# Softcap attention and two MLPs on one core: another order of the first matmuls' end products, differences of their outputs taken inside them, and another order of the first attention steps

## The chip, the cores and the metric

The kernel runs on one core of one Trainium2 chip. The time is the device time of one execution in microseconds (us); the median of three runs of the kernel before is 1092.13 us (1091.44 to 1093.55). The trace comes from one profiled execution that took 1090.3 us, of which the span of the recorded instructions is 1087.7 us.

In the profile PE is the matmul engine (PEld its weight loads), DVE the vector engine, ACT the scalar engine, POOL and SP the two engines that here mostly issue transfers (DMAs).

## The reference

```python
def _attn_ref(q, k, v, cap):                    # q, k, v: (4, 12, 448, 64)
    scores = (1.0 / np.sqrt(64)) * np.matmul(q, k.transpose(0, 1, 3, 2))
    scores = cap * np.tanh(scores / cap)
    scores = scores - np.max(scores, axis=-1, keepdims=True)
    attn = np.exp(scores)
    attn = attn / (np.sum(attn, axis=-1, keepdims=True) + 1e-09)
    return np.matmul(attn, v)

def _moe_ref(x, w_in, w_out):                   # (1792, 768) x (768, 2048) x (2048, 768)
    h = np.maximum(x @ w_in, 0.0)
    return h * h @ w_out

def _moe2_ref(x, w_in, w_out):
    h = x @ w_in
    return (h * (1.0 / (1.0 + np.exp(-1.702 * h)))) @ w_out
```

The attention's output, laid out as 4 x 448 tokens by 12 x 64 columns, goes through the first and then the second of these layers. All data are 32-bit floats.

## The kernel before, in words

Every matmul input is split into a high and a low part, and a product is the sum of three matmuls: high by high, high by low, low by high. The splits are made on the chip: ACT copies the high part (of a weight `wh`, L1120; of an activation `form`, L1152), and DVE subtracts it for the low part (`wl`, L1121; `form`, L1153).

**Attention** takes 12 quads (two pairs of heads each) in four steps each, 48 steps in all, written out by `attn_step(s)`: transposes of q and k (`qps`, `kps`), scores (`sps`, L834), tanh (`tanhs`, ACT L847), exponentials (`exps`, ACT L851), and the sums over v of quads before (`vxps`, `vyps`, L867). `attn_loads(s)` issues the loads on the SP queue by the table LOADS (L1532), where a larger first number is an earlier step. Loads take a rotating buffer, so a load is also held until its buffer's last reader is done. While attention runs, weights for the layers are unpacked from the inputs' own format and written to scratch in memory; POOL's queue loads them (`wraw`) and writes them (`wsa`, `wsb`), SP's queue later reads them back (`wf`).

**The layers.** For each layer l (0, 1) and each pair of batches c (0, 1) there is a first matmul "a" (768 to 2048) and a second "b" (2048 to 768). Each is done in a form of matrix multiplication with seven products where the direct one has eight; the seven products' inputs are sums and differences of blocks, called forms. So "a" is 56 products (s, o), with s the form (1 to 7) and o the column block (0 to 7), of nine matmuls each; "b" is 21 products of 24 matmuls. PE runs a(0,0), b(0,0), a(0,1), b(0,1), a(1,0), b(1,0), a(1,1), b(1,1), one after the other; the first matmuls stand at 234 to 338, 446 to 546, 653 to 756 and 868 to 971 us. The first two products of b are interleaved with the last two of a.

**Around a product.** For product u the program writes: what is in the list `later` (DVE work, flushed just ahead of the product), the nine or 24 matmuls, the split of the weights of four products further on (W_AHEAD), a step of making forms (`x_step` for the next or current "a", `b_step` for "b"), then `after(u)`, which takes the outputs from PSUM, adds them up and applies the layer's curve, and last a slot of the background unpacking (A_WORK, B_WORK, in chunks). `in_order` (L1391) keeps this written order on every engine, so an instruction that waits also holds everything written behind it on its engine. The seven forms rotate in seven buffers.

**Forms of "a".** `x_step(l, c, 0)` to `(l, c, 4)` run in the last products of the b before. Steps 5, 6 and 7 (forms 3, 2 and 4) follow products k = 0, 1 and 2 of the new "a", whose products begin (1,0), (5,0), (6,0), (2,0), (7,0), (1,1). Each form is 128x1344: an ACT copy and a DVE subtraction.

**Forms of "b".** The outputs of "a" are the blocks g11, g12, g21 and g22. `b_step` makes the forms of b from them in three chunks of columns (1344, 1344, 896 wide), with wide DVE subtractions (L1269). The first form of each chunk is written behind products (5,7), (6,7) and (2,7) of "a", after their `after`.

**The start.** Step 0 writes the scores of both pairs, then both tanhs, then transposes of the second quad's k and q, where the q's (`qps`) wait until the k's (`kps`) have been read out of their PSUM bank, and only then the scores of step 1. The scalar `capt` comes by a DMA of ACT's own queue, ahead of ACT's q loads.

Of the kernel before, what the change touches and what calls it, by code (L numbers as in the profile page):

```python
# [677 lines left out]
def bounded_cap(ctx, tc, q, k, v, cap, w1, w2, w3, w4, out, over):  # L678

    nc = tc.nc  # L680
# [212 lines left out]

    def start_pair(b, p):
        prep_q(b, p, transposed(raw[b, p, "q"], "qps", ps_m.tile([P, 512], F32, tag="m", name="qps")))
        prep_k(b, p)

    def attn_step(s):
# [7 lines left out]
        for i, x in enumerate(now):  # L906
            if s == 0 and i:
                start_pair(*x)
            scores(*x, c)
            if c == TAIL and ahead:  # L910

                t = raw[(*ahead[0][1], "q" if i else "k")]
                more.append(transposed(t, "qps" if i else "kps", sc[(*x, c)][:, 1]))
        for x in now:
            tanhs(*x, c)
        for f, ps in zip((prep_k, prep_q), more):
            f(*ahead[0][1], ps)
        if s == 0:
            prep_k(*ahead[0][0])
# [9 lines left out]
        if c == 0 and ahead:  # L929
            prep_q(*ahead[0][0])  # L930
# [142 lines left out]
    def a_products(l, c):  # L1073
        for o in range(NJ):
            yield (1, o)
            yield (5, o)
            if o:
                yield (4, o - 1)
            yield (6, o)
            if o:  # L1080
                yield (3, o - 1)
            yield (2, o)
            yield (7, o)
# [139 lines left out]
    def x_step(l, c, step):  # L1223
# [15 lines left out]
        if step == 0:  # L1239
            get("t", left, 0)  # L1240
            get("u", right, 0)
            get("w", right, NX)
        elif step == 1:
            form(1, "t")
            sub("t", "u", "t")
        elif step == 2:
            form(5, "t")
            sub("u", "w", "u")
        elif step == 3:
            form(7, "u")  # L1250
            later.append(lambda: get("u", left, NX))
            sub("t", "w", "t")
        elif step == 4:
            form(6, "t")
        elif step == 5:
            form(3, "w")
        elif step == 6:
            form(2, "u")
            sub("t", "u", "t")
        else:  # L1260
            form(4, "t")

    def b_step(l, c, s, ch):
# [4 lines left out]
        def sub(o, x, y):  # L1268
            later.append(lambda: v_.tensor_tensor(o, x, y, ALU.subtract))  # L1269

        def form(src):
            split_form((l, c, "b", s, ch), src, n)

        if s == 1:
            form(g11)
        elif s == 2:
            form(g21)
            sub(g11, g12, g11)
            t = gt["t", ch] = wide("tl")[:, :n]
            sub(t, g22, g11)  # L1280
        elif s == 6:
            form(gt["t", ch])
            sub(g12, g22, g12)
        elif s == 7:
            form(g12)
            sub(g21, g21, gt.pop(("t", ch)))
        elif s == 4:
            form(g21)
        elif s == 5:
            form(g11)  # L1290
        else:
            form(g22)
# [47 lines left out]

    def after(u):
# [19 lines left out]
        elif s == 7:  # L1361
            keep("u3", ps("b"))
            if kind == "a":
                g = gt["22"][:, i]
                plus("u3", ps("e"), g)
                curve(l, g)
# [4 lines left out]
        elif s == 3 and kind == "a":  # L1371
            g = gt["12"][:, i]
            plus("u2", ps("e"), g)
            curve(l, g)
# [27 lines left out]
    nc.vector.memset(kz[0][:, TAIL], 0.0)  # L1402
    for t in kz[1:]:
        nc.gpsimd.memset(t[:, TAIL], 0.0)
    nc.scalar.dma_start(out=capt, in_=cap.rearrange("(o n) -> o n", o=1).to_broadcast([P, 1]))
# [47 lines left out]
    for u, (l, c, kind, s, i) in enumerate(seq):  # L1453
# [4 lines left out]
        product(u)  # L1458
        if u == 0:
# [19 lines left out]
        if kind == "b" and n < 7:  # L1479
            b_step(l, c, order[n], i)  # L1480
        after(u)
        k = place[kind]
        place[kind] += 1
        if kind == "a":
            if i == NJ - 1 and s in (5, 6, 2):
                b_step(l, c, 1, (5, 6, 2).index(s))
# [4 lines left out]
            elif k < 3:  # L1491
                x_step(l, c, k + 5)
# [3 lines left out]
            if w0 <= k < 7 * NJ - 2:  # L1496
                weight_slots(k - w0, 7 * NJ - 2 - w0, m)
# [34 lines left out]
LOADS = ((8, "q", 0), (8, "k", 1), (7, "q", 1), (10, "k", 0), (1, "v", 0), (1, "v", 1))  # L1532
KB = 4
QB = 3
RAWQ = lambda nc: nc.gpsimd
W_AHEAD = 4
A_WORK = {(0, 0): 17 - ATT_CHUNKS, (0, 1): 6, (1, 0): 7}
# [46 lines left out]
```

## Time and profile before

| what | us |
|---|---|
| median of three runs | 1092.13 (1091.44 to 1093.55) |
| the profiled execution | 1090.3 |
| its span of recorded instructions | 1087.7 |
| PE busy | 1050.3 (97%) |
| DVE busy | 825.1 (76%) |
| ACT busy | 685.3 (63%) |
| POOL busy | 279.9 (26%) |

The difference of 2.6 us between the profiled execution and its span lies ahead of the first and behind the last recorded instruction. PE is busy for all but 37 us of the span; idle time is counted from the modelled end of the matmul before. Read the layers by stage: a stage lasts 85 to 120 us, and inside it PE waits only at a few places.

### The profile page before, as it was taken

How to read it: one execution, taken by the hardware profiler on the slowest of the kernel's cores; microseconds unless marked ns; L12 is line 12 of the kernel's file. 1: busy time of each engine (PE TensorE's matmuls, PEld its weight loads, DVE VectorE, ACT ScalarE, POOL GpSimd, SP SyncE). 2: the span in 40 equal slices, each digit the busy share in tenths (PEclk: the TensorE clock that was granted, in tenths of full speed). 3: DMA queues.
4: the chain of work that ended last, by engine and by line, in shares of the span. 5: the costliest groups of instructions: out<-in, count | busy, mean ns of one | idle time of the engine just before them, and what ended most of it. 6: DMA issues, size and time to landing. Idle time of an engine off the chain costs nothing.

```text
span 1087.7 us, 17044 instructions
## 1 busy us (share of the span) xinstructions
PE 1050.3 (97%) x5887; PEld 865.8 (80%) x5887; DVE 825.1 (76%) x1156; ACT 685.3 (63%) x1072; POOL 279.9 (26%) x422
## 2 busy tenths in 40 slices
PE   6999989999999999999999999999899999999997
PEld 4444534468999999899999998999899889998996
DVE  2686888876879976966798777878994975579854
ACT  5887869975767565566765646667555455564551
POOL 1223333322541022123202313442113400001033
PEclk9999999999999999999999999999999999999999
DMA  5798898956996487688846767997344543333443
GB/s 115 201 285 245 262 284 247 290 174 189 364 331 211 150 274 260 213 285 292 297 142 218 245 236 236 303 312 235 129 140 142 177 133 103 119 107 119 132 124 72
DMA packets 149616, 228.36 MB, mean 210 GB/s; under 512 B 65600, under 2 KB 102592, under 8 KB 149520
## 3 DMA queue, kind: packets, MB, share of 16 engines
q0 software_dynamic: 36768, 122.32, 34.2%
q1 hardware_dynamic: 110512, 104.29, 32.0%
q8 instruction: 48, 0.79, 0.3%
q10 hardware_dynamic: 2240, 0.57, 0.3%
q14 instruction: 48, 0.39, 0.1%
HBM read 166.53 MB, written 60.56 MB: 209 GB/s over the span
## 4 chain that ended last, share of the span: by engine, by line
PE 63%; issue 14%; DVE 10%; DMA 7%; POOL 4%; ACT 2%; ACTq 0%; DVEq 0%; POOLq 0%
PE pa L1144 30%; PE pb L1144 29%; DMA xs<-x 4%; DVE form L1153 3%; DVE wl L1121 2%; PE sps L834 1%; POOL wsa L995 1%; DMA wf<-wsa 1%; DMA out_dram<-o 1%; DMA xl<-ys 1%; POOL wraw L964 1%; POOL xs L892 1%; DVE g L1269 1%; DVE g L1354 1%; ACT form L1152 1%
## 5 line engine op out<-in xcount | busy, mean ns | idle before, releaser
L1144 PE MATMUL pa<-form,wh 128*128 128x448 f32 x1536 | 440.1, 367 | 5.7 <-DVE form L1153 4.8
L1144 PE MATMUL pb<-form,wh 128*128 128x448 f32 x1152 | 330.8, 368 | 1.6 <-ACT qu L1351 1.1
L1144 PEld LDWEIGHTS pa<-form,wh 128*128 128x128 f32 x1536 | 288.4, 188 | 34.1 <-DVE form L1153 6.0
L1144 PE MATMUL pa<-form,wl 128*128 128x448 f32 x768 | 282.5, 368 | 6.1 <-DVE wl L1121 6.1
L1120 ACT ACTIVATE wh<-wf 128x384 fp32r<-128x384 f32 (+1 forms) x392 | 211.2, 559 | 62.8 <-DMA wf<-wsa 21.7
L1121 DVE TENSOR_TENSOR wl<-wf,wh 128x384 fp32r<-128x384 f32 (+1 forms) x392 | 225.4, 606 | 18.3 <-ACT wh L1120 17.6
L1144 PEld LDWEIGHTS pb<-form,wh 128*128 128x128 f32 x1152 | 216.9, 188 | 23.1 <-ACT qu L1351 1.8
L1144 PE MATMUL pb<-form,wl 128*128 128x448 f32 x576 | 211.7, 367 | 0.0
L1144 PEld LDWEIGHTS pa<-form,wl 128*128 128x128 f32 x768 | 144.4, 188 | 21.8 <-DVE wl L1121 9.1
L1334 POOL DMA_DIRECT2D out_dram<-o x92 | 57.9, 636 | 252.6 <-DVE o L1332 249.3
L1144 PEld LDWEIGHTS pb<-form,wl 128*128 128x128 f32 x576 | 108.4, 188 | 9.8
L1153 DVE TENSOR_TENSOR form<-g,form 128x1344 fp32r<-128x1344 f32 (+1 forms) x72 | 100.7, 1399 | 9.4 <-ACT form L1152 8.7
L847 ACT ACTIVATE e<-sps 128x896 f32<-128x896 f32 (+1 forms) x96 | 75.0, 825 | 33.4 <-PE sps L834 29.1
L1351 ACT ACTIVATE qu<-pb 128x448 f32<-128x448 f32 x88 | 47.6, 541 | 70.4 <-PE pb L1144 67.8
L1152 ACT ACTIVATE form<-g 128x1344 fp32r<-128x1344 f32 (+1 forms) x72 | 85.8, 1192 | 2.0 <-DVE g L1308 1.9
L980 DVE SCALAR_TENSOR_TENSOR wy<-wraw,sx 128x768 int32<-128x768 int32 (+1 forms) x68 | 61.6, 907 | 32.7 <-ACT sx L976 30.3
L851 ACT ACTIVATE e<-e,ecap 128x896 f32<-128x896 f32 (+1 forms) x96 | 85.9, 952 | 0.0
L834 PE MATMUL sps<-qq,kk 64*128 64x448 f32 (+1 forms) x504 | 77.4, 396 | 1.4 <-ACT kk L812 1.4
L834 PEld LDWEIGHTS sps<-qq,kk 64*128 64x128 f32 (+1 forms) x504 | 51.5, 193 | 33.8 <-ACT e L847 10.3
L976 ACT ACTIVATE sx<-wraw 128x768 f16<-128x768 bf16 (+1 forms) x68 | 69.6, 1024 | 1.9 <-DVE wy L980 1.3
L964 POOL DMA_DIRECT2D wraw<-in_moe_w_out_dram x72 | 53.3, 744 | 54.0 <-DVE wy L980 26.4
L1354 DVE SCALAR_TENSOR_TENSOR g<-pa,qu 128x448 f32<-128x448 f32 x64 | 39.8, 622 | 33.2 <-PE pa L1144 17.1
(113 smaller groups left out, 1025.9 us busy)
## 6 DMA issues: line engine op xcount, KB each, us to landing
wf<-wsa SPq DMA_DIRECT2D x224, 192.0 KB, 3.9
wf<-wsb SPq DMA_DIRECT2D x168, 256.0 KB, 3.1
wraw<-in_moe_w_in_dram POOLq DMA_DIRECT2D x32, 766.5 KB, 7.5
wraw<-in_moe_w_out_dram POOLq DMA_DIRECT2D x48, 383.2 KB, 6.1
wsa<-wy POOLq DMA_DIRECT2D x32, 384.0 KB, 4.7
wsb<-wy POOLq DMA_DIRECT2D x24, 384.0 KB, 4.9
wsa<-ws POOLq DMA_DIRECT2D x16, 384.0 KB, 5.2
wraw<-in_moe_w_out_dram POOLq DMA_DIRECT2D x24, 255.5 KB, 6.0
```

What stands on the lines that cost most here:

```text
L834: nc.tensor.matmul(ps[:, u, :S], x, y, start=all(t[0] != u for t in todo[:n]), stop=all(t[0] != u for t in todo[n + 1 :]),)
L847: a_.activation(e, chunk(c, sc.pop((b, p, c)))[:, :, :S], AF.Tanh)
L851: a_.activation(e, e, AF.Exp, scale=ecap)
L964: raw_queue[0].dma_start(out=t.bitcast(U8)[:, h * m : h * m + m, : 8 * P - 2], in_=src.rearrange("(k p) f -> p k f", p=P),)
L976: a_.activation(z, words(BF16)[:, :, :, 2], AF.Copy)
L980: v_.scalar_tensor_tensor(y[:, : 2 * n].bitcast(I32), words(I32)[:, :, :, 0], 13, sx[:, : 2 * n], ALU.logical_shift_right, ALU.bitwise_or,)
L1120: a_.activation(x, src, AF.Copy)
L1121: later.append(lambda: v_.tensor_tensor(y, src, f32(x), ALU.subtract))
L1144: nc.tensor.matmul(ps[:, :S], a[:, kk % 4, :], r, start=(s in (1, 5) and kk == 0 and n == 0), stop=(kk == ks - 1 and n == 2), skip_group_c ...
L1152: a_.activation(f[:, 0, :n, :], src, AF.Copy)
L1153: later.append(lambda: v_.tensor_tensor(f[:, 1, :n, :], src, f32(f[:, 0, :n, :]), ALU.subtract))
L1334: nc.gpsimd.dma_start(out=out[b * S : (b + 1) * S, m * P + 32 * j : m * P + 32 * j + 32].rearrange("(c p) d -> p c d", p=32), in_=o[32 * j ...
```

## The change

- Step 0 of attention: the tanhs of the first pair are written ahead of the second pair's transposes; the transposes of the second quad's k go to a spare PSUM bank, and that quad's q transposes move to the end of step 1. `capt` is loaded by POOL's queue.
- LOADS has 2 instead of 1 for v.
- `a_products` begins and ends in another order; `x_step` makes form 2 (then 4, then 3) at k = 1, 3 and 5.
- The curves of g22 and g12 are written one product later (`soon`); g12 becomes g22 - g12 there, block by block (`shaped`), and `b_step` changes one wide difference accordingly at s = 2 and s = 6.
- The first forms of b are written directly behind products (6,7), (2,7) and (3,6), ahead of the weight split.
- Background slots of "a" end at product 50 (W_END) instead of 54; a(0,1) does 7 chunks instead of 6, a(1,0) 6 instead of 7.

```diff
@@ -891,8 +891,11 @@
             v_.tensor_tensor(x, x, r, ALU.mult)
             Q_PUT.dma_start(out=to[i], in_=x)
 
+    def spare():
+        return ps_m.tile([P, 512], F32, tag="m", name="qps")
+
     def start_pair(b, p):
-        prep_q(b, p, transposed(raw[b, p, "q"], "qps", ps_m.tile([P, 512], F32, tag="m", name="qps")))
+        prep_q(b, p, transposed(raw[b, p, "q"], "qps", spare()))
         prep_k(b, p)
 
     def attn_step(s):
@@ -907,16 +910,18 @@
             if s == 0 and i:
                 start_pair(*x)
             scores(*x, c)
+            if s == 0 and not i:
+                tanhs(*x, c)
             if c == TAIL and ahead:
 
                 t = raw[(*ahead[0][1], "q" if i else "k")]
                 more.append(transposed(t, "qps" if i else "kps", sc[(*x, c)][:, 1]))
-        for x in now:
+        for x in now[s == 0 :]:
             tanhs(*x, c)
         for f, ps in zip((prep_k, prep_q), more):
             f(*ahead[0][1], ps)
         if s == 0:
-            prep_k(*ahead[0][0])
+            prep_k(*ahead[0][0], transposed(raw[(*ahead[0][0], "k")], "kps", spare()))
         if c == TAIL and len(ahead) > 1:
             kps = transposed(raw[(*ahead[1][0], "k")], "kps")
         for m, part, at in PV[c]:
@@ -926,7 +931,7 @@
             exps(*x, c)
         if c == TAKE and 0 < n <= len(quads):
             take(n - 1)
-        if c == 0 and ahead:
+        if c == (0 if n else 1) and ahead:
             prep_q(*ahead[0][0])
         if c == TAIL and len(ahead) > 1:
             prep_k(*ahead[1][0], kps)
@@ -1071,16 +1076,14 @@
         return f
 
     def a_products(l, c):
-        for o in range(NJ):
-            yield (1, o)
-            yield (5, o)
-            if o:
-                yield (4, o - 1)
-            yield (6, o)
-            if o:
-                yield (3, o - 1)
-            yield (2, o)
-            yield (7, o)
+
+        yield from ((1, 0), (5, 0), (6, 0), (1, 1), (7, 0), (2, 0), (5, 1), (4, 0), (6, 1), (3, 0), (2, 1), (7, 1))
+        for o in range(2, NJ):
+            yield from ((1, o), (5, o), (4, o - 1), (6, o))
+            if o < NJ - 1:
+                yield from ((3, o - 1), (2, o), (7, o))
+            else:
+                yield from ((2, o), (7, o), (3, o - 1))
 
     seq = []
     for l in range(2):
@@ -1253,37 +1256,37 @@
         elif step == 4:
             form(6, "t")
         elif step == 5:
-            form(3, "w")
-        elif step == 6:
             form(2, "u")
             sub("t", "u", "t")
+        elif step == 6:
+            form(4, "t")
         else:
-            form(4, "t")
+            form(3, "w")
 
     def b_step(l, c, s, ch):
 
         k0, n = CHUNKS[ch]
         g11, g12, g21, g22 = (gt[x][:, k0 : k0 + n] for x in ("11", "12", "21", "22"))
 
-        def sub(o, x, y):
-            later.append(lambda: v_.tensor_tensor(o, x, y, ALU.subtract))
-
         def form(src):
             split_form((l, c, "b", s, ch), src, n)
+
+        def put(o, x, y, op=ALU.subtract):
+            later.append(lambda: v_.tensor_tensor(o, x, y, op))
+
 
         if s == 1:
             form(g11)
         elif s == 2:
             form(g21)
-            sub(g11, g12, g11)
             t = gt["t", ch] = wide("tl")[:, :n]
-            sub(t, g22, g11)
+            put(t, g12, g11, ALU.add)
         elif s == 6:
             form(gt["t", ch])
-            sub(g12, g22, g12)
+            put(g11, g22, gt["t", ch])
         elif s == 7:
             form(g12)
-            sub(g21, g21, gt.pop(("t", ch)))
+            put(g21, g21, gt.pop(("t", ch)))
         elif s == 4:
             form(g21)
         elif s == 5:
@@ -1338,6 +1341,12 @@
                 in_=o[32 * j : 32 * j + 32],
             )
 
+    soon = []
+
+    def shaped(l, i, g):
+        curve(l, g)
+        v_.tensor_tensor(g, gt["22"][:, i], g, ALU.subtract)
+
     def after(u):
         l, c, kind, s, i = seq[u]
 
@@ -1363,7 +1372,7 @@
             if kind == "a":
                 g = gt["22"][:, i]
                 plus("u3", ps("e"), g)
-                curve(l, g)
+                soon.append(lambda: curve(l, g))
         elif s == 2 and kind == "a":
             curve(l, gt["11"][:, i], ps("a"))
         elif s == 4 and kind == "a":
@@ -1371,7 +1380,7 @@
         elif s == 3 and kind == "a":
             g = gt["12"][:, i]
             plus("u2", ps("e"), g)
-            curve(l, g)
+            soon.append(lambda: shaped(l, i, g))
         elif s in (2, 4):
             t = small("t", 2)
             a_.activation(t, ps("a" if s == 2 else "b"), AF.Copy, scale=scale)
@@ -1400,9 +1409,9 @@
 
     first = len(nc.cur_bb.bb.instructions)
     nc.vector.memset(kz[0][:, TAIL], 0.0)
+    nc.gpsimd.dma_start(out=capt, in_=cap.rearrange("(o n) -> o n", o=1).to_broadcast([P, 1]))
     for t in kz[1:]:
         nc.gpsimd.memset(t[:, TAIL], 0.0)
-    nc.scalar.dma_start(out=capt, in_=cap.rearrange("(o n) -> o n", o=1).to_broadcast([P, 1]))
     for x in quads[0]:
         load_k(*x)
         load_q(*x)
@@ -1456,6 +1465,9 @@
             place = {"a": 0, "b": 0}
         flush()
         product(u)
+        first_b = ((6, NJ - 1), (2, NJ - 1), (3, NJ - 2))
+        if kind == "a" and (s, i) in first_b:
+            b_step(l, c, 1, first_b.index((s, i)))
         if u == 0:
             hi, lo = wt[0]
             for n in range(3):
@@ -1478,23 +1490,24 @@
             x_step(*nxt, 0)
         if kind == "b" and n < 7:
             b_step(l, c, order[n], i)
+        now, soon[:] = list(soon), []
         after(u)
+        for f in now:
+            f()
         k = place[kind]
         place[kind] += 1
         if kind == "a":
-            if i == NJ - 1 and s in (5, 6, 2):
-                b_step(l, c, 1, (5, 6, 2).index(s))
             m = A_WORK.get((l, c), 0)
             if (l, c) == (0, 0):
                 for n in X_LATE.get(k, ()):
                     x_rest(n)
-            elif k < 3:
-                x_step(l, c, k + 5)
+            elif k in X_LAST:
+                x_step(l, c, 5 + X_LAST.index(k))
             w0 = W_AT if (l, c) == (0, 0) else 5
             if k == w0 - 2:
                 weight_group(m)
-            if w0 <= k < 7 * NJ - 2:
-                weight_slots(k - w0, 7 * NJ - 2 - w0, m)
+            if w0 <= k < W_END:
+                weight_slots(k - w0, W_END - w0, m)
         else:
             (t0, t1), m = B_WORK.get((l, c), ((0, 0), 0))
             if m and k == t0:
@@ -1529,12 +1542,14 @@
 X_LATE = {2: (4,), 3: (5,), 4: (6,), 5: (7,)}
 W_AT = 10
 RAW_AT = (0, 1, 2, 3)
-LOADS = ((8, "q", 0), (8, "k", 1), (7, "q", 1), (10, "k", 0), (1, "v", 0), (1, "v", 1))
+LOADS = ((8, "q", 0), (8, "k", 1), (7, "q", 1), (10, "k", 0), (2, "v", 0), (2, "v", 1))
 KB = 4
 QB = 3
 RAWQ = lambda nc: nc.gpsimd
+W_END = 50
+X_LAST = (1, 3, 5)
 W_AHEAD = 4
-A_WORK = {(0, 0): 17 - ATT_CHUNKS, (0, 1): 6, (1, 0): 7}
+A_WORK = {(0, 0): 17 - ATT_CHUNKS, (0, 1): 7, (1, 0): 6}
 B_WORK = {(0, 0): ((8, 14), 2), (0, 1): ((8, 14), 2)}
 
 
```

The first place is PE's order at the start of the program. `qps` and `kps` are the transposes of q and k, `sps` the scores; kz_117 is the k of the second quad. Before:

```order
L804 MATMUL qps<-ident,qt 128x112 x4
L804 MATMUL kps<-ident,kz_116 128x128 x4
L834 MATMUL sps<-qq,kk 128x448 x6
L804 MATMUL kps<-ident,kz_117 128x128 x4
L804 MATMUL qps<-ident,qt 128x112 x4
L834 MATMUL sps<-qq,kk 128x448 x24
L867 MATMUL vsps<-e,ones 32x448 x8
```

Now:

```order
L804 MATMUL qps<-ident,qt 128x112 x4
L804 MATMUL kps<-ident,kz_116 128x128 x4
L834 MATMUL sps<-qq,kk 128x448 x6
L804 MATMUL qps<-ident,kz_117 128x128 x4
L834 MATMUL sps<-qq,kk 128x448 x12
L804 MATMUL qps<-ident,qt 128x112 x4
L834 MATMUL sps<-qq,kk 128x448 x12
```

The twelve scores of step 1 now stand ahead of the second quad's q transposes, and the k transposes go into another bank (a `qps` tile).

The second place is SP's queue where v is loaded, after the first quads: `qt`, `kz` and `vz` are loads of q, k and v. These rows stand in both programs, in this order:

```order
L787 DMA qt<-in_q_dram 112x4x64 x2
L779 DMA kz_117<-in_k_dram 128x3x64 x2
L781 DMA kz_117<-in_k_dram 64x64 x2
L792 DMA vz_121<-in_v_dram 128x2x192
L797 DMA vz_121<-in_v_dram 64x64 x2
L792 DMA vz_122<-in_v_dram 128x2x192
L797 DMA vz_122<-in_v_dram 64x64 x2
```

Nothing on SP's queue moves anywhere in the program: its 1139 rows are the same in both.

The third place is DVE's order at the start of a(0,1). `form` is the low part of a form, `wl` that of a weight, `xl` a difference that goes into a later form, `qu` and `g` are sums of outputs. Before:

```order
L1153 TENSOR_TENSOR form<-xl,form 128x1344
L1121 TENSOR_TENSOR wl<-wf,wh 128x384 x2
L1153 TENSOR_TENSOR form<-xl,form 128x1344
L1121 TENSOR_TENSOR wl<-wf,wh 128x384
L1153 TENSOR_TENSOR form<-xl,form 128x1344
L1237 TENSOR_TENSOR xl<-xl 128x1344
L1121 TENSOR_TENSOR wl<-wf,wh 128x384
L1153 TENSOR_TENSOR form<-xl,form 128x1344
```

Now:

```order
L1156 TENSOR_TENSOR form<-xl,form 128x1344
L1124 TENSOR_TENSOR wl<-wf,wh 128x384 x3
L1156 TENSOR_TENSOR form<-xl,form 128x1344
L1240 TENSOR_TENSOR xl<-xl 128x1344
L1124 TENSOR_TENSOR wl<-wf,wh 128x384 x2
L1156 TENSOR_TENSOR form<-xl,form 128x1344
L1363 SCALAR_TENSOR_TENSOR g_4794<-pa,qu_4894 128x448
```

The first `form` of each piece is form 6. Before, form 3, form 2 and form 4 follow it, one in each product; now form 2 comes next, and form 4 and form 3 follow with two products' weights between them.

The fourth place is DVE's order where b(0,1) begins; `tl` is the chunk's difference that becomes form 6. Before:

```order
L1153 TENSOR_TENSOR form<-g_4788,form 128x1344
L1269 TENSOR_TENSOR g_4786<-g_4787,g_4786 128x1344
L1269 TENSOR_TENSOR tl<-g_4789,g_4786 128x1344
L1121 TENSOR_TENSOR wl<-wf,wh 128x384
L1121 TENSOR_TENSOR wl<-wf,wh 128x512 x2
```

Now:

```order
L1348 TENSOR_TENSOR g_4792<-g_4794,g_4792 128x448
L1124 TENSOR_TENSOR wl<-wf,wh 128x512
L1156 TENSOR_TENSOR form<-g_4793,form 128x1344
L1275 TENSOR_TENSOR tl<-g_4792,g_4791 128x1344
L1124 TENSOR_TENSOR wl<-wf,wh 128x384
L1124 TENSOR_TENSOR wl<-wf,wh 128x512 x2
```

One wide difference of each chunk is gone there; in its place a difference of 448 columns (L1348) follows each g12.

## Rows read from the trace of the kernel before

**Rows 1.** PE's waits by what ended them: line, releaser: us in all, times, longest.

```profile
PE vxps L867 <- DMA vz<-in_v_dram: 6.9, 3, 4.4
...
PE pa L1144 <- DVE wl L1121: 6.1, 8, 1.6
...
PE pa L1144 <- DVE form L1153: 4.8, 3, 2.0
...
PE pa L1144 <- ACT form L1152: 0.8, 2, 0.6
```

**Rows 2.** Timeline of the start: start, us, engine, instruction [idle before <- releaser].

```profile
0.75 0.40 ACTq L1405 DMA_DIRECT2D capt<-in_cap_dram  x1
...
1.18 4.16 ACTq L787 DMA_DIRECT2D qt<-in_q_dram  x4
...
14.09 0.92 ACT L847 ACTIVATE e<-sps 128x896 f32<-128x896 f32 x1 [0.77 <-PE sps L834]
14.90 1.96 ACT L851 ACTIVATE e<-e,ecap 128x896 f32<-128x896 f32 x2
...
19.10 0.92 ACT L847 ACTIVATE e<-sps 128x896 f32<-128x896 f32 x1 [2.23 <-PE sps L834]
```

**Rows 3.** Timeline of PE where it waits longest for v.

```profile
99.58 0.73 PE L867 MATMUL vxps<-e,vz 128*32 128x448 f32 x2 [2.31 <-DMA vz<-in_v_dram]
...
157.97 0.96 PE L867 MATMUL vxps<-e,vz 128*32 128x448 f32 x2 [4.36 <-DMA vz<-in_v_dram]
```

**Rows 4.** Timeline of PE and DVE at the starts of first matmuls.

```profile
449.93 1.56 DVE L1153 TENSOR_TENSOR form<-xl,form 128x1344 fp32r<-128x1344 f32 x1
...
451.87 1.55 DVE L1153 TENSOR_TENSOR form<-xl,form 128x1344 fp32r<-128x1344 f32 x1
...
453.48 0.47 PE L1144 MATMUL pa<-form,wh 128*128 128x448 f32 x1 [1.43 <-DVE form L1153]
453.79 0.37 PE L1144 MATMUL pa<-form,wl 128*128 128x448 f32 x1
...
876.86 0.47 PE L1144 MATMUL pa<-form,wh 128*128 128x448 f32 x1 [1.97 <-DVE form L1153]
```

**Rows 5.** Timeline of PE where second matmuls begin.

```profile
565.61 0.47 PE L1144 MATMUL pa<-form,wl 128*128 128x448 f32 x1 [0.39 <-DVE wl L1121]
...
769.74 0.47 PE L1144 MATMUL pa<-form,wl 128*128 128x448 f32 x1 [1.63 <-DVE wl L1121]
...
777.88 0.47 PE L1144 MATMUL pa<-form,wl 128*128 128x448 f32 x1 [1.20 <-DVE wl L1121]
...
991.28 0.47 PE L1144 MATMUL pa<-form,wl 128*128 128x448 f32 x1 [0.99 <-DVE wl L1121]
```

**Rows 6.** DVE by stretch: stretch, length, busy (instructions), PE's granted clock, DMA share, GB/s.

```profile
546.00:565.00 19.00, 18.83 (x24) 1.00 0.45 149
```

**Rows 7.** DVE's differences for form 6 of b: duration ns min/median/max, starts, shapes.

```profile
L1269 DVE TENSOR_TENSOR tl<-g,g x12: 1091/1557/1560, 346.8 to 994.5; 128x1344 f32<-128x1344 f32 x8, 128x896 f32<-128x896 f32 x4
```

**Rows 8.** Engines by stretch: PE, PEld, DVE, ACT, POOL busy, clock, DMA share, GB/s.

```profile
878.10:881.50 3.40, 3.40 (x11) 3.00 (x10) 2.48 (x4) 2.58 (x4) 0.00 (x0) 0.50 0.20 58
```

**Rows 9.** The same columns: two of a(0,0), one of a(0,1), attention.

```profile
253.00:272.00 19.00, 17.46 (x83) 15.20 (x83) 10.03 (x19) 8.97 (x18) 8.09 (x12) 1.00 0.80 252
...
253.00:336.00 83.00, 81.47 (x393) 73.33 (x393) 60.73 (x110) 55.47 (x101) 38.99 (x55) 1.00 0.93 318
...
455.00:541.00 86.00, 86.00 (x426) 79.69 (x425) 61.77 (x107) 59.47 (x109) 23.25 (x32) 1.00 0.88 295
...
40.00:210.00 170.00, 161.84 (x1408) 79.50 (x1401) 136.09 (x186) 141.41 (x182) 59.74 (x84) 0.98 0.92 265
```

**Rows 10.** The page's GB/s in 40 equal slices of the span.

```profile
GB/s 115 201 285 245 262 284 247 290 174 189 364 331 211 150 274 260 213 285 292 297 142 218 245 236 236 303 312 235 129 140 142 177 133 103 119 107 119 132 124 72
```

**Rows 11.** The chain of waits in two first matmuls: start, us, engine, tile, matmuls.

```profile
457.19 3.65 PE pa L1144 x18
...
664.78 3.72 PE pa L1144 x18
```

## Prediction

> **What bounds the kernel now.** I read the engines' shares first, then PE's waits, then the timeline around each wait, then the windows by stage. PE is busy for 97% of the span, the matmuls of the layers run back to back, and the change leaves their number as it is: what it can win are PE's stops, and what it can lose are new ones. The table of waits sorts the stops [rows 1]: v's loads 6.9 us, low parts of weights 6.1, low and high parts of forms 4.8 and 0.8. The reader is to see in the timelines that these stand in few places: the start of attention [rows 2], two takes of v [rows 3], the starts of the three first matmuls behind the first one [rows 4], and the beginnings of second matmuls [rows 5]. So I price each place by itself.
>
> A stop costs more than its idle column. A matmul's row lasts 0.37 us, but the next starts 0.203 us after it (3.65 us for 18 [rows 11]), so 0.16 of a stop lie inside the row ahead; and the second start after the stop at 453.48 comes 0.31 later instead of 0.203 [rows 4], 0.11 more. I add 0.27 us to each stop that goes.
>
> **The start.** ACT sits idle 2.23 us until 19.10, waiting for the scores of step 1; its two exponentials are over at 16.86 [rows 2]. Before, those scores stand behind the transposes of the second quad's k and q in PE's order, and the q's wait for a bank. Now the scores come first and the k's have a bank of their own: the tanh can follow the exponentials directly, 2.23. The tanh at 14.09 still needs the second pair's scores, so its 0.77 stays. `capt` leaves ACT's queue, where it took 0.40 ahead of the q loads at 1.18 that the first transposes need: 0.40. Sum 2.6. At worst one tanh of 0.92 still falls behind (1.7), at best the 0.77 goes too (3.4). POOL now issues one more load ahead of its memsets, which nothing reads before v is first used; and the second quad's q transposes only fall due at step 4. Is all of this time at the end? Attention is a chain over ACT and PE from the first step on, but with a DMA share of 0.92 from 40 to 210 us [rows 9] and PE waiting for v [rows 3], part of it could be given back: 0 to 3.4, I take 2.6.
>
> **v.** The table asks for v a step sooner, but SP's queue is the same, row for row. An instruction can't move past the one ahead of it, and each load also waits for the buffer's last reader. I cost it at nothing: the stops at 99.58 and 157.97 stay. Bounds: 0, and the 6.9 us of all v waits.
>
> **Starts of first matmuls.** Product (2,0) is fourth in a(0,1) and waits for form 2. DVE makes form 3's low part at 449.93 and form 2's only at 451.87, and PE starts 0.1 after it, with 1.43 idle at 453.48 [rows 4]. Three stops of this kind make the 4.8 us, and ACT's high part two shorter ones, 0.8 [rows 1]. Now form 2 comes directly after form 6, and its product is sixth: two products of 1.83 us later and one form of 1.55 sooner, 5.2 us of room against at most 1.97 of wait. Forms 4 and 3 come at k = 3 and 5, products (4,0) and (3,0) are eighth and tenth: four products of time each. All five stops go: 4.8 + 0.8 + 5 x 0.27 = 7.0. What is late next is nothing of DVE's: it is busy 61.8 of 86 us in a(0,1) [rows 9]. If form 2 merely halves its wait, 3.5.
>
> [...]
>
> **Where second matmuls begin.** DVE is busy 18.83 of 19 us from 546 to 565 [rows 6], and the low parts of weights come late: four stops, 0.39, 1.63, 1.20 and 0.99 [rows 5], with 4 x 0.27 5.3 us. In each of the first three b products DVE had a form's low part (1.55), two wide differences of 1.56 [rows 7] and weights, more than the product's 24 x 0.203 = 4.87 us. Now one wide difference less stands there, 1.56 in each; over the three products (two at 1344, one at 896) that is 4.2 us, more than any of the stops. The first forms are also written ahead of the outputs' sums of "a". I take 5.3 as won; bounds 0 (the differences return at s = 7, later in the same stage) and 5.3.
>
> The difference goes into "a" as eight of 448 columns. From 1344 to 896 a wide one falls from 1557 to 1091 ns [rows 7], 0.466 for 448, so one of 448 is some 0.62, an estimate; eight are 5.0 against 4.2, 0.8 us more of DVE in each first matmul. DVE has 24 us to spare in a(0,1) [rows 9], so I take nothing; the most it can cost is 4 x 0.8 = 3.2. [...]
>
> **Denser background work.** Slots of "a" now end at product 50. In a(0,0) the same seven chunks go into 40 products instead of 44: of 318 GB/s [rows 9] some 106 are the weights read for the products themselves (a tile of 128x384 values of 4 bytes in each product of 1.86 us), the other 212 become 233, in all 340. In a(0,1) seven chunks instead of six go into 45 products instead of 49: 295 [rows 9] less 106 is 189, times 7/6 and 49/45 is 240, in all 346. The page's slices show 364 GB/s in the slice from 272 to 299 us [rows 10], and PE's idle time from 253 to 336 (1.53 us) is all of it from before 272 (1.54) [rows 9]: at that rate nothing stopped. So it fits, narrowly. I take one more stretch as bad as 253 to 272, 1.54 + 3 x 0.27 = 2.3, as +2; bounds 0 and nine such stretches over a(0,0) and a(0,1) (169 of 19 us), +21.
>
> **Sum.** -2.6 - 7.0 - 1.7 - 5.3 + 2 = -14.6. The profiled execution took 1090.3, so 1075.7; the median of the runs is 1.8 above it: 1077.5.
>
> **The pace of matmuls.** 18 matmuls take 3.65 in one stretch and 3.72 in another [rows 11], both at full clock. With 4032 layer matmuls the difference of 3.9 ns is 15.7 us between all at one and all at the other. What sets it I can't see; it holds from one stop to the next, so with other stops it will be dealt anew. With half of them at each now, that is up to 8 either way, more likely 4.
>
> **Rivals.**
> 1. Slower: the transfers saturate. If 340 to 346 GB/s cannot be held while the products' weights are read, unpacked chunks come late, POOL, DVE and ACT hold the forms behind them in their written order, and a(0,0) and a(0,1) stop as in 253 to 272. It decides once the DMA share asked for passes 1.0; by the share (0.93 for 318, 0.88 for 295) the new rates would take 0.99 and 1.03. -16.6 + 21 = +4.4: 1096.5. For it: those shares. Against: the slice at 364.
> 2. The loads of v do come sooner, its three stops go and the time falls by 6.9 + 3 x 0.27 = 7.7 more, to about 1070. For it: the waits are on these very loads. Against: SP's identical order.
> 3. DVE stays late where second matmuls begin, since the new small differences fall due in the last products of "a" while ACT and DVE also make b's first forms: the 5.3 isn't won, 1083. For it: 18.83 of 19 busy. Against: 4.2 us less in those products.
> 4. The start is given back later in attention, which waits for DMAs: 1080.
>
> **How the numbers follow.** Forecast 0.66, rivals 0.08, 0.06, 0.11 and 0.09. The forecast's own range, with the pace at 4 and the starts' and clock's bounds, is 1072 to 1084; rivals 2 to 4 and the pace's ends take it to 1068 to 1088, which leaves out most of rival 1. A measurement can tell this kernel from no change from 0.2% on, 2.2 us. Rival 1 gives slower at its full price, 0.05, and no change at half of it, 0.03; of the other cases 0.01 is left for each of these. Faster 0.90, same 0.04, slower 0.06.
>
> **What would show it.** Right: ACT starts the third tanh at about 16.9 - 0.4; v's waits as before; no wait for form L1156 in the first products of "a", no 0.50 stretch around 878; at most one wait for `wl` of over 0.3 us in the first six products of each b. Wrong: stops strewn through a(0,0) and a(0,1) at a DMA share near 1.0 (rival 1), v's waits gone (rival 2), `wl` waits of 1 us at the same products (rival 3), attention's end no earlier (rival 4). Matmuls at another pace in a whole stage would move the time without any stop.

## The result and the profile after

The changed kernel takes 1073.13 us (median of four runs, 1071.62 to 1074.54) against 1091.79 of before (four runs, 1089.55 to 1093.55): ratio 0.983, 95% interval 0.9807 to 0.9853, so 1.7% faster. Forecast were 1077.5 and 1068 to 1088. The profiled execution took 1074.54 us, its span 1072.7.

PE's waits after, as [rows 1] has those of before (line, releaser: us in all, times, longest):

```profile
PE vxps L867 <- DMA vz<-in_v_dram: 8.4, 4, 3.5
...
PE pb L1147 <- ACT pb L1367: 2.5, 1, 2.5
PE pa L1147 <- DVE wl L1124: 1.4, 3, 0.7
...
PE pa L1147 <- DVE form L1156: 0.4, 2, 0.2
```

Forms cost PE 0.4 us instead of 4.8 and 0.8, weights 1.4 instead of 6.1. v's waits, which this change was to shorten by its table, are 8.4 instead of 6.9. New is one wait of 2.5 in a(0,0).

The start, on ACT (start, us, engine, instruction), answering [rows 2]:

```profile
14.50 1.97 ACT L851 ACTIVATE e<-e,ecap 128x896 f32<-128x896 f32 x2
16.37 1.71 ACT L847 ACTIVATE e<-sps 128x896 f32<-128x896 f32 x2
```

The third tanh starts at 16.37 without a wait, where it stood at 19.10 after 2.23 of waiting: 2.73 sooner, of which 0.40 come from `capt` leaving ACT's queue (the exponentials start at 14.50 instead of 14.90).

The start of a(0,1) on DVE, answering [rows 4]:

```profile
442.37 1.56 DVE L1156 TENSOR_TENSOR form<-xl,form 128x1344 fp32r<-128x1344 f32 x1
443.85 1.49 DVE L1124 TENSOR_TENSOR wl<-wf,wh 128x384 fp32r<-128x384 f32 x3
445.79 1.56 DVE L1156 TENSOR_TENSOR form<-xl,form 128x1344 fp32r<-128x1344 f32 x1 [0.46 <-ACT form L1155]
...
450.22 1.56 DVE L1156 TENSOR_TENSOR form<-xl,form 128x1344 fp32r<-128x1344 f32 x1 [0.46 <-ACT form L1155]
```

The forms now come 3.4 and 4.4 us apart with weights between them, and PE waits for none. By stretch (length; PE, PEld, DVE, ACT, POOL busy; clock; DMA share; GB/s), answering [rows 9]:

```profile
253.00:331.00 78.00, 74.67 (x367) 68.44 (x366) 59.24 (x111) 53.22 (x97) 37.77 (x53) 1.00 0.97 337
455.00:535.00 80.00, 80.00 (x389) 72.67 (x388) 65.05 (x117) 55.39 (x101) 28.96 (x40) 1.00 0.99 346
```

The rates forecast were 340 and 346 GB/s. a(0,1) carries 346 with PE busy all the time; a(0,0) loses 3.3 us.

**Where the 15 us came from.** I split the layers by the starts of their 4032 matmuls. What a start lies later than 0.2027 us after the one before is pace if it lies within 0.22, half clock between 0.36 and 0.38, and otherwise a stop. In every run 0.6 us of a(0,0)'s stops are no stop but three further matmuls that run there and aren't among the 4032.

| us | before | after | difference | forecast |
|---|---|---|---|---|
| first layer matmul (the start, attention) | 234.13 | 231.37 | -2.8 | -2.6 |
| stops in a(0,0) | 3.83 | 4.63 | +0.8 | +2 |
| stops in the other first matmuls | 8.44 | 1.13 | -7.3 | -7.0 |
| stops in second matmuls | 6.81 | 2.48 | -4.3 | -5.3 |
| half clock | 1.54 | 0 | -1.5 | -1.7 |
| pace | 7.98 | 8.20 | +0.2 | 0, up to 8 either way |
| outside the span | 2.6 | 1.8 | -0.8 | 0 |

Together -15.7, against 15.8 between the two profiled executions. The medians differ by 18.7; the rest is what one execution differs from another, below. The first row above all compares one trace with one: that start varies by 10 us in the same program.

### The profile page after: what moved, and what is told of

It is laid out like the page before. It is cut to its first block, busy times and chain, and to the rows that moved or that the text cites. A ratio compares the mean times of both kernels' runs of the same rounds, so it can differ in the third digit from the quotient of the medians.

```text
span 1072.7 us, 17090 instructions
## 1 busy us (share of the span) xinstructions
PE 1044.3 (97%) x5887; PEld 863.5 (81%) x5887; DVE 823.8 (77%) x1176; ACT 686.4 (64%) x1072; POOL 281.0 (26%) x423
## 4 chain that ended last, share of the span: by engine, by line
PE 83%; DMA 8%; issue 5%; POOL 1%; DVE 1%; ACT 1%; SPq 0%; ACTq 0%; POOLq 0%; DVEq 0%
PE pa L1147 39%; PE pb L1147 32%; PE sps L834 4%; DMA vz<-in_v_dram 4%; PE vxps L867 2%; PE vyps L867 2%; PE vsps L867 2%; DMA qt<-in_q_dram 1%; DMA out_dram<-o 1%; DMA wraw<-in_moe_w_out_dram 1%; DMA xl<-ys 1%; PE qps L804 1%; POOL xs L892 0%; PE sps L804 0%; PE kps L804 0%
## 5 line engine op out<-in xcount | busy, mean ns | idle before, releaser
L1124 DVE TENSOR_TENSOR wl<-wf,wh 128x384 fp32r<-128x384 f32 (+1 forms) x392 | 227.7, 606 | 21.4 <-ACT wh L1123 21.0
L867 PE MATMUL vxps<-e,vz 128*32 128x448 f32 x384 | 52.6, 550 | 8.4 <-DMA vz<-in_v_dram 8.4
```

The costliest lines, as they stand in the source:

```text
L867: nc.tensor.matmul(ps[32 * i : 32 * i + 32, :S], x, t, start=c == 0, stop=c == TAIL, skip_group_check=True,)
L1124: later.append(lambda: v_.tensor_tensor(y, src, f32(x), ALU.subtract))
```

## The experiments

All are the changed kernel with an edit. The same program varies: the layers' start lies between 231.4 and 241.0 us over the ten runs below whose attention is the changed kernel's (all but e2, e7 and e10; mean 236.0, standard deviation 2.9), and the pace costs 0.2 to 9.3 us. So a few us in the layers are read from the trace, by the split above:

| run | median us | ratio to before | layers start | pace | half clock | stops a(0,0) | other "a" | all "b" |
|---|---|---|---|---|---|---|---|---|
| before | | 1 | 234.1 | 8.0 | 1.5 | 3.8 | 8.4 | 6.8 |
| changed | 1073.13 | 0.983 | 231.4 | 8.2 | 0 | 4.6 | 1.1 | 2.5 |
| e1, v's table | 1078.30 | 0.9888 | 236.8 | 4.7 | 0 | 4.4 | 1.1 | 2.6 |
| e2, old start | 1078.82 | 0.9889 | 238.4 | 5.5 | 2.6 | 5.2 | 1.1 | 2.4 |
| e3, old starts of "a" | 1088.02 | 0.9948 | 235.0 | 6.7 | 4.3 | 5.4 | 9.1 | 2.1 |
| e4, wide differences | 1076.81 | 0.9867 | 231.4 | 7.5 | 1.5 | 4.8 | 1.0 | 3.7 |
| e5, old first forms | 1079.95 | 0.9871 | 241.0 | 5.6 | 0 | 5.0 | 1.2 | 2.2 |
| e6, old slots | 1076.71 | 0.9853 | 238.1 | 1.7 | 0 | 3.8 | 1.6 | 4.0 |
| e7, v really first | 1082.73 | 0.9897 | 247.8 | 4.1 | 2.4 | 5.3 | 2.4 | 2.6 |
| e8, slots 14 to 54 | 1075.91 | 0.9856 | 235.9 | 4.0 | 0 | 2.4 | 2.5 | 3.8 |
| e9, e4 and e5 | 1081.96 | 0.9881 | 236.6 | 9.3 | 0 | 5.2 | 1.3 | 3.6 |
| e10, slow start | 1087.49 | 0.9921 | 246.4 | 9.4 | 0 | 5.1 | 1.1 | 2.5 |
| e11, slots 14 to 50 | 1078.45 | 0.9833 | 237.8 | 5.4 | 0 | 4.9 | 1.5 | 2.5 |
| e12, e9 and e6 | 1075.88 | 0.9863 | 236.0 | 0.2 | 0 | 2.9 | 1.1 | 3.8 |

**e1, v's table back.**

> The changed kernel with 1 again instead of 2 for v in the table of loads. My theory: the table's entry moves no instruction on any engine, so the time is that of the changed kernel, 1073 us, within what two timings of one program differ (2 us), and PE's waits for v stay near 8 us. Rival (the loads of v do come sooner): the time rises, and PE's waits for v fall back to 6.9 us or change place by more than in a second run of the same program.

```diff
-LOADS = ((8, "q", 0), (8, "k", 1), (7, "q", 1), (10, "k", 0), (2, "v", 0), (2, "v", 1))
+LOADS = ((8, "q", 0), (8, "k", 1), (7, "q", 1), (10, "k", 0), (1, "v", 0), (1, "v", 1))
```

Instruction for instruction this is the changed kernel; SP's 605 transfers stand in one order in the traces of before, the changed kernel and e1. Its ratio is 0.9888 (0.9858 to 0.9918), 0.6% above the first comparison's 0.983 on another chip: so much two timings of one program differ here, and more than the 2 us I had expected. v's waits were 10.3 us. The table's entry does nothing.

**e2, the old start.**

```diff
-            if s == 0 and not i:
-                tanhs(*x, c)
-        for x in now[s == 0 :]:
+        for x in now:
...
-            prep_k(*ahead[0][0], transposed(raw[(*ahead[0][0], "k")], "kps", spare()))
+            prep_k(*ahead[0][0])
...
-        if c == (0 if n else 1) and ahead:
+        if c == 0 and ahead:
```

> The changed kernel with the old order of the first attention steps; the scalar capt stays on POOL's queue. Theory (the 2.2 us that ACT stood idle before the third tanh were on the path to the end): +2.2 us, 1075.3; the first matmul of the layers starts 2.2 us later than the changed kernel's 231.4. Rival (attention waits for transfers and gives the start's gain back): no difference in the time, the first matmul of the layers at 231.4 within 0.6.

```profile
14.50 1.96 ACT L851 ACTIVATE e<-e,ecap 128x896 f32<-128x896 f32 x2
18.70 0.92 ACT L847 ACTIVATE e<-sps 128x896 f32<-128x896 f32 x1 [2.23 <-PE sps L834]
```

The third tanh waits 2.23 us again, and starts at 18.70; the exponentials before it stay at 14.50, so the 0.40 is `capt`'s. The layers start 2.4 us later than the ten runs' mean, with a spread of 2.9, and the median is 0.5 above e1's. That decides nothing about the end; hence e10.

**e10, a slow start.** In step 1 the first pair's tanh runs eleven times.

```diff
+        for _ in range(11 if (b, p) == quads[0][0] and c == 1 else 1):
+            a_.activation(e, ps, AF.Tanh)
```

> The changed kernel, with the tanh of the first pair in step 1 done eleven times over into the same tile, which holds ACT about 8 us longer at 17 us and changes no output. Theory (what ACT gains or loses at the start reaches the end in full): +8 us, the first matmul of the layers at 240 to 249, 8 us above the 231.4 to 241 of seven runs with the same attention (mean 235.6), the time 1084 to 1087. Rival (attention is bound by its transfers, and a delay at the start is taken back while PE and ACT would have waited for v and q): +4 us or less, PE's waits for v and q fall by as much as is taken back.

```profile
16.44 11.20 ACT L849 ACTIVATE e<-sps 128x896 f32<-128x896 f32 x12
```

The twelve tanhs take 11.20 us where two take 1.71, so the delay is 9.5. The layers start at 246.4, 10.4 above the mean of 236.0, and the median is 9.0 above e11's, which shared its chip. That is the theory's range for the layers' start, and the median lies 0.5 above the theory's range for the time. PE's waits for v and q are 17.2 us in all, against 15.1 in the changed kernel's profile and 18.3 in e11's. But e9 shared the chip too, and the median is only 5.5 above its; and between the start and the layers the delay doesn't stay whole. Starts of some of attention's 96 tanhs in us (e10's ten extra ones not counted):

| tanh | before | e2, old start | the ten runs | their mean | e10 |
|---|---|---|---|---|---|
| 3rd | 19.1 | 18.7 | 16.3 to 16.7 | 16.5 | 16.4 |
| 13th | 39.0 | 38.6 | 35.9 to 36.3 | 36.1 | 46.8 |
| 25th | 64.2 | 63.8 | 61.1 to 68.3 | 64.6 | 72.0 |
| 41st | 104.6 | 104.4 | 100.5 to 106.3 | 102.7 | 106.0 |
| 96th | 228.0 | 232.3 | 225.2 to 234.8 | 229.9 | 240.3 |

e10 is 10.7 us late at the 13th tanh, 3.3 at the 41st and 10.5 at the 96th: part was given back on the way, as the rival has it, and PE's waits for v from 121 us on made it late again. So the medians show that more than the rival's 4 us of the delay reach the end, but not that all of it does. What the start saves is there in each of the ten runs up to the 13th tanh, and gone in e2. Behind it the ten runs lie 6 to 10 us apart, with before and e2 among them: that the 2.7 us reach the end is not shown.

**e3, the old starts of the first matmuls.**

```diff
-X_LAST = (1, 3, 5)
+X_LAST = (0, 1, 2)
...
-        yield from ((1, 0), (5, 0), (6, 0), (1, 1), (7, 0), (2, 0), (5, 1), (4, 0), (6, 1), (3, 0), (2, 1), (7, 1))
-        for o in range(2, NJ):
+        yield from ((1, 0), (5, 0), (6, 0), (2, 0), (7, 0))
+        for o in range(1, NJ):
```

(and `x_step` makes forms 3, 2, 4 again).

> The changed kernel with the old order of products at the start of each first matmul and with forms 3, 2 and 4 made at products 0, 1 and 2 as before. Theory: PE waits for form 2 again at the starts of a(0,1), a(1,0) and a(1,1), 5 stops of 5.6 us with their restarts 7.0 us, and the stretch at clock 0.50 comes again behind the third: +7 to +8.7 us, 1080 to 1082. Rival (the stops at these starts went because DVE has less to do in the products before, not because of the order): under +2 us, and no wait for a form above 0.5 us there.

```profile
452.85 0.47 PE L1147 MATMUL pa<-form,wh 128*128 128x448 f32 x1 [1.43 <-DVE form L1156]
...
661.32 0.47 PE L1147 MATMUL pa<-form,wh 128*128 128x448 f32 x1 [1.44 <-DVE form L1156]
...
875.90 0.47 PE L1147 MATMUL pa<-form,wh 128*128 128x448 f32 x1 [1.98 <-DVE form L1156]
```

The two stops of [rows 4] and the third, 1.44 at 661.01 before, are back to within 0.01 us, with both short ones, and the stops of these first matmuls rise by 8.0 us. The clock surprised me. Columns here: length, PE busy, clock, DMA share, GB/s:

```profile
454.30:457.20 2.90, 2.90 (x9) 0.50 0.89 261
662.60:665.50 2.90, 2.90 (x9) 0.50 0.83 263
877.50:880.40 2.90, 2.90 (x9) 0.50 0.24 68
```

All three stops are followed by a stretch at the lower level, which before only the third was. The order of the starts is worth 9.7 us by the medians of e3 and e1, more than any other part and above the theory's 8.7, by that clock.

**e4, the wide differences back.**

```diff
-            put(t, g12, g11, ALU.add)
+            put(g11, g12, g11)
+            put(t, g22, g11)
...
-            soon.append(lambda: shaped(l, i, g))
+            soon.append(lambda: curve(l, g))
```

> The changed kernel with the two wide differences per chunk back in the first products of each second matmul, and no differences of 448 columns in the first matmuls; the first forms of b stay where the change writes them. Theory (the lack of 1.56 us of DVE work per product is what took the waits for weights away): waits for low parts of weights of 1 to 1.6 us come again in the first six products of the second matmuls behind the first, in all +3 to +5.3 us, 1076 to 1078.4. Rival (the earlier writing of the first forms and the order of the last products did it): under +1 us, no such wait above 0.3 us.

Two waits, 0.80 in b(1,0) and 0.79 in b(1,1); the second matmuls' stops rise by 1.2, neither the theory's 3 to 5.3 nor the rival's under 1. The median is 1.5 below e1's.

**e5, the old place of the first forms and the old end of "a".**

```diff
-        if kind == "a" and (s, i) in first_b:
-            b_step(l, c, 1, first_b.index((s, i)))
...
+            if i == NJ - 1 and s in (5, 6, 2):
+                b_step(l, c, 1, (5, 6, 2).index(s))
...
-                yield from ((2, o), (7, o), (3, o - 1))
+                yield from ((3, o - 1), (2, o), (7, o))
```

> The changed kernel with the first forms of each second matmul written where they were before (behind products (5,7), (6,7), (2,7), after their sums), and the old order of the last products of each first matmul; the differences of 448 columns inside the first matmuls stay. The run with the wide differences back (e4) gave only two waits of 0.80 us for weights there. Theory now (the earlier place of the first forms and the order of the last products took most of the waits away): waits for weights or forms of 0.4 to 1.6 us come again in the first products of the second matmuls of (0,1), (1,0) and (1,1), in all stops of +2.5 to +4 us in the trace of the layers. Rival (either of the two edits alone is enough): stops within 1 us of the changed kernel's 8.2.

2.2 us in the second matmuls, no more than in the changed kernel: the rival, as if either edit were enough.

**e9, the edits of e4 and e5 together.**

> The changed kernel with both edits around the second matmuls undone: the wide differences back in their first products, and the first forms and the order of the last products of each first matmul as before. Each edit undone alone left nearly no stop there (1.4 us and 0.1 us more than with both). Theory (either edit is enough by itself): with neither the four stops of before come back, stops of the layers +4 to +5.5 us over the changed kernel's 8.2, 1077 to 1084 in time. Rival (the stops went because of the other starts of the first matmuls or the other slots): within 2 us of 8.2.

3.6 us in the second matmuls, with 0.66 at 768.0 us in b(1,0) and 0.80 at 977.6 in b(1,1). So both together do no more than e4's edit. The places tell more. Of the stops of [rows 5], the 1.63 at 769.74 stands in (3,7), the last product of "a" among b's first; the other three, 0.39, 1.20 and 0.99, stand at the third matmul of b's fourth product. The stops of e4 and e9 are all in (3,7), in b(1,1) too, where before had none there. At the other place neither has one, nor has any other run of the changed kernel. So the wide differences bring back about half of the 1.63, and e12's expectation below, which takes the 0.80 of b(1,1) for the 0.99 of before, compares two places. The three stops in b's fourth product went for another reason.

**e12, the edits of e9 and the old slots.** To e9:

```diff
-W_END = 50
+W_END = 54
-A_WORK = {(0, 0): 17 - ATT_CHUNKS, (0, 1): 7, (1, 0): 6}
+A_WORK = {(0, 0): 17 - ATT_CHUNKS, (0, 1): 6, (1, 0): 7}
```

> As e9 (wide differences, place of the first forms and last products as before), and besides the background slots end at product 54 again, with six chunks in a(0,1) and seven in a(1,0). Left of the change around the second matmuls is only that the curves are written a product later. In e9 the waits of before came back at b(1,1) (0.80 for 0.99), but not in full at b(1,0) (0.66 for 1.63 and 1.20) and not at b(0,1) (0 for 0.39). Theory (the unpacking that DVE does in the last products of a(0,1) and a(1,0), which a(1,1) doesn't have, is what made the difference): waits of 1.8 us or more in all at the start of b(1,0), 0.3 or more at b(0,1), 0.8 at b(1,1); stops of the layers 11.5 to 14. Rival (the waits between ACT and DVE in the curves made it): stops as in e9, 10.1, within 0.7.

```profile
759.02 0.47 PE L1144 MATMUL pa<-form,wl 128*128 128x448 f32 x1 [0.80 <-DVE wl L1121]
```

0.80 at b(1,0), 0.79 at b(1,1), both in (3,7) again, none at b(0,1) and none in a fourth product: unpacking in the last products isn't the reason either. All stops are 7.8 us, outside a(0,0) 4.9 as in e9. What is left of the change there is `soon`. Before, ACT in b(1,0):

```profile
775.99 0.58 ACT L1307 ACTIVATE qt<-g 128x448 f32<-128x448 f32 x1 [6.67 <-DVE g L1354]
776.47 0.61 ACT L1120 ACTIVATE wh<-wf 128x512 fp32r<-128x512 f32 x1
```

The tanh of a curve waits 6.67 us for the sum that DVE makes behind its wide differences, and the weights' high part, written behind it, waits along; PE stops at 777.88 for 1.20 [rows 5]. In e12, at the same place of the program:

```profile
758.81 0.62 ACT L1120 ACTIVATE wh<-wf 128x512 fp32r<-128x512 f32 x1
761.71 0.64 ACT L1120 ACTIVATE wh<-wf 128x512 fp32r<-128x512 f32 x1 [2.27 <-DMA wf<-wsb]
```

With the curve written a product later ACT waits only for the weight's transfer, and that stop is gone. Every other part but the move of `capt` was undone in one of e1 to e6, and those three stops in b's fourth product never came back. But no run undid `soon` itself, so this is read from the traces and by elimination, not shown by an edit.

**e6, the old slots alone** (e12's two lines, nothing else).

> The changed kernel with the background slots of the first matmuls ending at product 54 again, six chunks in a(0,1) and seven in a(1,0). Theory (the denser transfers cost nothing since PE stops in a(0,1) not at all, and the stops of a(0,0) come from what is loaded at its products 8 to 13): stops of a(0,0) and a(0,1) within 0.5 us of the changed kernel's 4.6 and 0. Rival (the denser slots cost the forecast's 2 us in a(0,0)): a(0,0)'s stops fall to 3.5 us or less. If the end at 50 served the second matmuls, their stops rise.

a(0,0)'s stops are 3.8 here and 2.9 in e12, against 4.4 to 5.4, mean 5.0, in the nine runs with slots from 10 to 50: the denser slots cost 1.2 to 2.1 us there. e6 alone lies between the theory's 4.1 and the rival's 3.5. a(0,1) has 0.1 more. In return the second matmuls lose 1.6 more with the old slots, 0.80 of it in one wait for a form at the start of b(1,0). That is what the end at 50 serves beside the early first forms; e12, which writes them where before did, has no such wait.

**e8, slots 14 to 54; e11, 14 to 50** (the first line alone).

```diff
-W_AT = 10
+W_AT = 14
-W_END = 50
+W_END = 54
```

> The changed kernel with the background slots of a(0,0) from product 14 instead of 10 and to 54 instead of 50, so that the first unpacked loads are issued four products later than the last two writes of attention's outputs. Theory (a(0,0)'s stops of 4.6 us come from weights of the products that queue behind those writes and the four loads issued with them, 2.4 us of latency becoming 10): a(0,0)'s stops fall to under 2 us. Rival (the same loads collide with the products' weights wherever they start): 4 us or more, later by four products.

> The changed kernel with the background slots of a(0,0) from product 14 instead of 10, and all slots still ending at product 50. The run with 14 to 54 (e8) had 2.2 us less of stops in a(0,0), but 1.9 us more around the starts of the second matmuls and in a(0,1). Theory (those came from the end at 54, the gain from the start at 14): a(0,0)'s stops under 2.5 us, the other stops as in the changed kernel, in all 5.5 to 6.5 us instead of 8.2. Rival (seven chunks in 36 products ask more of the queues than they carry): a(0,0)'s stops 4 us or more.

In a(0,0) of the changed kernel ACT waits 4.13 us at 257.6 for a weight's read and 3.00 at 261.6 for `wraw`; both were issued within about 2 us of attention's last two writes. In e8 a(0,0) stops for 2.4 us, between theory and rival, but the other first matmuls and the second ones lose 1.3 more each. In e11 a(0,0) stops for 4.9, the rival. Neither is below the changed kernel in all.

**e7, v's loads really earlier.**

```diff
-LOADS = ((8, "q", 0), (8, "k", 1), (7, "q", 1), (10, "k", 0), (2, "v", 0), (2, "v", 1))
+LOADS = ((8, "q", 0), (8, "k", 1), (7, "q", 1), (2, "v", 0), (2, "v", 1), (10, "k", 0))
```

> The changed kernel with v's loads moved ahead of the next quads' k loads in the table, so that they really stand earlier on SP's queue, about 4 us at each quad. Theory (PE waits for v because its load is issued too late on a busy queue): PE's waits for v fall from 7 to 10 us to under 4 us and the layers start 3 to 6 us sooner than in the runs with the same attention (231.4 to 236.8), and the time falls by 2 to 5 us. Rival (attention is bound by the transfers as a whole, share 0.92): the waits move to k or q loads, and the layers start no sooner than 231.

```profile
PE kps L804 <- DMA kz<-in_k_dram: 21.5, 5, 7.5
PE qps L804 <- DMA qt<-in_q_dram: 5.8, 1, 5.8
```

v's waits vanish and k's take their place, 21.5 us; the layers start at 247.8. Here the queue's order only chose which load is late. No run points to a version that beats the changed kernel beyond this spread.

## Why the prediction was right

The sum, -14.6, was nearly met by the two profiles (-15.7) and by e1 on its chip (-13.9); the first comparison's medians differ by 18.7. Several terms met their size better than their reason.

- **The start**: 2.6 forecast, 2.73 at the third tanh, and still there in all ten runs at the 13th. The 2.8 at the first layer matmul is luck: ten runs start the layers between 231.4 and 241.0, mean 236.0, and before's one trace at 234.1. Rival 4 stays open; e10 gave back part of its delay on the way. POOL's memsets behind `capt` hold up nothing, though not for the reason given: the first transposes read `ident`, which POOL has made by 3.0 us, and wait for q until 5.67.
- **v**: nothing, as forecast; e1 is the same program. Rival 2 fails even where v's loads really come sooner (e7): k's are late instead.
- **Starts of first matmuls**: -7.0 forecast, -7.3 measured, and e3 brings the stops back. The clock's 1.7 in the sum was my estimate, half of the 3.40 us at clock 0.50 [rows 8]. No run shows it; what the two traces show is 1.5, half clock of 1.54 us before and none in the changed kernel's layers. Nor is it tied to the stop of 1.97, as e3's theory had it: in e3 the stops of 1.43 and 1.44 are followed by the lower level as well, 4.3 in all.
- **Beginnings of second matmuls**: -5.3 forecast, -4.3 measured, and the reason failed for the larger part. The step "one wide difference less stands there, 1.56 in each" explains 1.2 us (e4), the early first forms nothing alone (e5), both together 1.1 (e9), with the slots 1.3 (e12); it is the stop in (3,7). Some 3 us, the three stops in b's fourth product with what follows them, are left to the late curves, which I had not priced at all. I had read DVE's 18.83 of 19 us busy [rows 6] as work that had to go; in b(1,0) it was also ACT held behind DVE by a curve.
- **Eight small differences for three wide**: one of 448 took 0.626 us (0.62 estimated), so eight take 5.0 for the three wide ones' 4.2. The bound of 3.2 us wasn't reached: PE doesn't stop in a(0,1) or a(1,0), and without the small ones (e4) the other first matmuls' stops are 1.0 for 1.1. So the 0.8 us more on DVE were off the path.
- **Denser background**: +2 forecast, +0.8 between the two profiles, 1.2 to 2.1 by e6 and e12. Rival 1's rates were reached, 337 and 346 GB/s at shares 0.97 and 0.99, and only a(0,0) stopped.
- **Pace**: +0.2 in this pair, by luck. It doesn't hold from one stop to the next, as the prediction says: see the last section.
- **Outside the span**: -0.8, which the sum didn't have.

## What to carry to other kernels

Where engines keep a written order, look at what stands behind a waiting instruction: a sum, a tanh and a product written in a row on two engines held the weights of a third, and, as far as the traces show, one product's delay freed them. Before crediting a change to a busy engine, undo the parts singly and together, and compare stops at the same product, not only their sums; here no part undone around the second matmuls brought back more than 1.6 of the 4.3 us. A gain near the start is worth following through the stage behind it: here waits for loads blur it within 60 us. And check that a table moves the queue at all before pricing what it moves.

## What the runs showed of the hardware

The layers' matmuls ran at two paces at full granted clock, 18 in 3.65 or 3.72 us [rows 11]; the same 4032 matmuls cost 0.2 us above the faster pace in e12 and 9.4 in e10. It also changed without a stop: a(0,1) of the changed kernel has none, and PE went there from 202.7 to 206.7 ns a matmul (start, us, engine, tile, matmuls):

```profile
429.89 14.19 PE pa L1147 x70
444.08 1.86 PE pb L1147 x9
```

What chooses the pace stays open.

A stop was followed by a stretch at the lower level (clock 0.50) only sometimes: the 1.43 at the start of a(0,1) wasn't before and was in e3; those of 2.5 to 3.0 in a(0,0) were in e2, e4 and e7 (2.6, 1.5 and 2.4 us of half clock) and weren't in the changed kernel, e1, e3, e5, e9 and e10. No stop under 1.4 us was in these traces.

The time outside the span, which I had taken as given, was 2.1 to 3.1 us in before's runs and 1.7 to 1.9 in all runs of the changed kernel and of e1 to e5 and e7 to e11. In e6 and e12, which alone have the old numbers of chunks, 6 and 7, it was 2.6 to 2.9 and 2.0 to 2.5. e8 also has the old end at 54, but not those numbers, and 1.8 to 1.9. So most of the 0.8 us goes with how the chunks are spread over the two stages; why, no trace shows, as the time lies outside it.
